# Two layers of linear attention and gated MLP on one core: key reciprocals by logarithm, half sums stored per head, and a written-out order of the work

## The chip, the cores and the metric

The kernel runs on one core of one Trainium2 chip. The time is the device time of one execution in microseconds (us), and lower is better. One execution was also recorded by the hardware profiler; its page and trace are called the profile here. The engines are PE (TensorE, matmuls), DVE (VectorE), ACT (ScalarE), POOL (GpSimd) and SP (SyncE, which here only issues DMAs).

## What is computed

The input x has 2048 rows of 512. Two identical layers follow one another, each an attention block and a gated MLP block, both with a normalisation in front and a residual sum behind. Cut to what matters (H = 32 heads of 16, F = 1376):

```python
q, k, v = heads(x @ wqkv)
pq, pk = q @ w_phi[h], k @ w_phi[h]
phi_q = concat([softmax(pq), softmax(-pq)])      # over the head's 16 features
phi_k = concat([softmax(pk), softmax(-pk)])
kv, z = phi_k.T @ v, phi_k.sum(over rows)        # sums over all 2048 rows
o = (phi_q @ kv) / (phi_q @ z + 1e-6)
x = x + heads_joined(o) @ wo
gate, up = xn @ W_gate, xn @ W_up
x = x + (relu(gate) * up) @ W_down
```

## The kernel before

The 2048 rows lie in 16 tiles of 128, four tiles to a chunk. X stays in SBUF throughout. `Plan` collects some 1800 operations with an engine, a cost, and what they read and write; an operation is one or several instructions. In the kernel before, `Plan.order` (line 99) then walks through simulated time: each engine takes, of its ready operations, the one with the highest rank (the longest remaining way to the end) plus a bias per group from the table `RANK`, as soon as the buffers are free. The order so found is emitted, and on the chip each engine works through its own list in order, waiting on semaphores. So the order on every engine is fixed when the program is built.

The stages of a layer, with the lines of the kernel before:

- **Loads** (lines 225 to 240): key and value weights and some of X on SP's queue, other parts of X, the feature weights and the query weights on ACT's. `load_weights` (line 294) issues the 28 parts of the output and MLP weights on SP.
- **Start** (`wake`, `feature_weights`): three matmuls of zeros (line 318), transposes of the key weight on PE (line 351), products with the feature weights (line 364), evacuated from PSUM by ACT (line 307) or DVE (line 309).
- **Normalisation** (`Norm`): statistics on DVE (lines 388, 390), the reciprocal root on POOL (lines 396, 398), the scaled tile on ACT (line 460), DVE or POOL (line 472), its transpose by DMA from SP (lines 486, 490) or on PE (line 481).
- **Keys and values** (`keys_values`): per tile four matmuls against the key weight (line 710), two exponentials on ACT (line 715; e to the x and e to the -x), their sums per head, the reciprocals of the sums on DVE (line 724), the scaling on POOL or DVE (line 730), the values (line 663, evacuated at 307 or 309), and eight narrow matmuls (line 752) that add the tile to the sums over rows. After the 16th tile DVE builds R from the sums (line 774).
- **Sums per head** (`feature_sums`): 64 numbers per head pair and sign are summed in groups of 16. A letter per tile chooses the way: "1" is one reduction of both signs on DVE (line 682), "2" two reductions (line 692), "H" and "P" let POOL first add the two halves of one or both signs (line 679), and DVE reduces the remainder (line 688).
- **Queries** (`queries`): matmuls (line 794), exponentials (line 798), sums, reciprocal (line 803), product of the reciprocals (line 807), scaling (line 814), transpose by DMA (line 816).
- **Attention** (`attention`): eight narrow matmuls per tile against R (line 833) into the one buffer `q`, a reciprocal (line 851) and a product (line 853) on DVE. That product is called the attention product here; there are 16 per layer. Then a transpose (line 860 or 866, by DMA; line 873 on PE), the output projection (line 884) and the residual sum on DVE (line 566).
- **MLP** (`Centre`, `glu`): centring on ACT or DVE (lines 524, 527), squares on ACT (line 548), transposes (lines 535, 539, 542), matmuls for gate and up (lines 593, 613), their evacuation and product on ACT and DVE (lines 598 to 630), the down projection (line 645), the residual sum (line 566 or, without a running total, 570), and in the last layer the output DMA (line 650). The last tile is stored in three pieces of 256, 128 and 128 columns.

Which engine does what for each tile stands in the strings of `STEP`. Two of its lines, as an example:

```python
    "kr0": "11H11HH11H2211H1", "kr1": "H22P11H2111222PP", "qr0": "21H1H11P2PH11212", "qr1": "112H121HH1HPP12P",
    "qs0": "DPPPDDPDPDPPDDPD", "qs1": "PDPPPPDDPDPPDPPP", "qq0": "DPPPDPDPPDPDDPDP", "qq1": "PPPPDDPDPDPPPPDP",
```

Of the kernel before, what the change touches and what calls it, by code (L numbers as in the profile page):

```python
# [8 lines left out]
P = 128  # L9
D = 512  # L10
H = 32
DH = 16
F = 1376
NDB = D // P
# [36 lines left out]
TAIL = {"PE": 0.165, "ACT": 0.12, "DVE": 0.115, "POOL": 0.045, "SP": 0.0}  # L51
SAME = {"PE": -0.165, "ACT": 0.035, "DVE": 0.035, "POOL": 0.08, "SP": 0.0}
HOPS = {("DVE", "POOL"): 0.09, ("ACT", "POOL"): 0.15}
NEXT = {"PE": 0.055, "SP": 0.03}
FREE = 0.06


def hop(a, b):
    return SAME[a] if a == b else HOPS.get((a, b), NEXT.get(b, 0.04))


class Plan:
# [10 lines left out]
    def op(self, eng, occ, fn, reads=(), writes=(), holds=(), lat=0.0, at=0.0, group=None, port=False, long=False):  # L73

        o = Op()
        o.eng, o.occ, o.cost, o.fn, o.lat, o.at, o.port, o.long = eng, occ, occ + TAIL[eng], fn, lat, at, port, long
        o.group, o.i_in = group or self.group
        base, slope = RANK.get(f"{o.group}.{eng}") or RANK[o.group]
        o.bias = base - slope * o.i_in
        o.preds, o.succs, o.i = set(), [], len(self.ops)  # L80
# [18 lines left out]
    def order(self):  # L99
        for o in self.ops:  # L100
            for p in o.preds:
                p.succs.append(o)
        for o in reversed(self.ops):
            o.rank = o.cost + o.lat + max([s.rank + hop(o.eng, s.eng) for s in o.succs], default=0.0)
        free = {k: [0.0] * n for k, (pool, n) in self.kinds.items()}
        engines = sorted({o.eng for o in self.ops})
        busy = {e: 0.0 for e in engines}
        ready = {e: [] for e in engines}
        for o in self.ops:
            o.wait, o.t0 = len(o.preds), o.at  # L110
            if not o.wait:
                ready[o.eng].append(o)
        seq, left, now, shut = [], len(self.ops), 0.0, 0.0
        while left:
            moved, later = False, []
            for e in engines:
                if busy[e] > now + 1e-9:
                    later.append(busy[e])
                    continue
                best = None  # L120
                for o in ready[e]:
                    if o.t0 > now + 1e-9:
                        later.append(o.t0)
                        continue
                    if o.port and shut > now + 1e-9:
                        later.append(shut)
                        continue
                    ok = True
                    need = {}
                    for b in o.bufs:  # L130
                        if b.slot is None:
                            need[b.kind] = need.get(b.kind, 0) + 1
                    for k, n in need.items():
                        got = [t for t in free[k] if t is not None]
                        if len(got) < n:
                            ok = False
                        else:
                            t = sorted(got)[n - 1]
                            if t > now + 1e-9:
                                later.append(t)  # L140
                                ok = False
                    if ok and (best is None or (o.rank + o.bias, -o.i) > (best.rank + best.bias, -best.i)):
                        best = o
                if best is None:
                    continue
# [5 lines left out]
                if o.long:  # L151
                    shut = end
# [856 lines left out]
```

## Time and profile before

| | |
|---|---|
| Median of 3 runs | 381.89 us (381.57 to 382.64) |
| The profiled execution | 380.91 us |
| Its span, first to last instruction | 379.2 us |
| Granted TensorE clock, mean | 0.999 |
| Busy: PE, DVE, ACT, POOL | 363.6, 268.0, 205.5, 121.1 us |
| DMA traffic | 32.61 MB, mean 86 GB/s |

In the rows of the profile, L12 is line 12 of the kernel of that run. A group's row has the line, the engine, the operation, what it writes and reads, shapes and count; then busy time, the mean time of one in ns, and the idle time before them with what ended it. A timeline's row has the start in us, the duration, the engine, the line, the operation and the count, and in brackets an idle time that preceded it. Successive instructions of an engine overlap a little, so the distance from one start to the next is what an instruction occupies; it is shorter than its duration. Buffer numbers are left out of names: `b` is any work buffer, `ps` a bank of PSUM.

### The profile page before, as it was taken

To read this page: it belongs to the slowest core of one execution; us is meant where nothing else is said; L and a number is where in the kernel's file an instruction comes from. 1 tells how busy PE (TensorE), PEld (TensorE's weight loads), DVE (VectorE), ACT (ScalarE), POOL (GpSimd) and SP (SyncE) were. 2 spreads that over 40 slices of the span, in tenths; PEclk is the share of its full clock that TensorE was granted. 3 is DMA by queue.
4 is the path that set the end of the run, shared out by engine and by line. 5 is a ranking of instruction groups with operands and counts; after the bars stand their busy time and mean duration, and the time that the engine had idled before them with its cause. 6 is when DMAs were issued, how large, how long until landed. Compare 5 with 4: busy or idle time off the path is not lost.

```text
span 379.2 us, 6724 instructions
## 1 busy us (share of the span) xinstructions
PE 363.6 (96%) x2380; PEld 189.9 (50%) x2409; DVE 268.0 (71%) x608; ACT 205.5 (54%) x439; POOL 121.1 (32%) x203
## 2 busy tenths in 40 slices
PE   4898999999899999999999999999999999999996
PEld 2444545756445444444444456475654445454444
DVE  4999999999925442763497998999962675172433
ACT  4898979776762446737706925865234135514100
POOL 3798965131110220560155681724310002000000
PEclk9999999999999999999999999999999999999999
DMA  8889936788950230021013070478930075000011
GB/s 262 239 143 227 260 44 144 133 149 146 145 107 2 42 58 15 0 30 27 0 22 77 9 119 3 87 127 146 171 85 14 5 146 115 14 0 16 1 55 57
DMA packets 98882, 32.61 MB, mean 86 GB/s; under 512 B 90560, under 2 KB 98336, under 8 KB 98848
## 3 DMA queue, kind: packets, MB, share of 16 engines
q1 hardware_dynamic: 97216, 29.93, 39.7%
q10 hardware_dynamic: 1632, 2.24, 1.8%
q8 instruction: 19, 0.31, 0.4%
q14 instruction: 15, 0.12, 0.1%
HBM read 8.44 MB, written 2.10 MB: 28 GB/s over the span
## 4 chain that ended last, share of the span: by engine, by line
PE 64%; DVE 24%; DMA 6%; issue 2%; ACT 1%; POOL 1%; SPq 0%; POOLq 0%; ACTq 0%
PE ps L613 37%; PE ps L645 14%; PE ps L884 5%; DMA b<-b 4%; DVE sk L682 4%; DVE rk L724 3%; DVE bnst L388 3%; PE ps L794 3%; PE ps L593 3%; DVE sk L692 2%; DVE b L730 2%; PE q L833 2%; DMA X<-in_A_x_dram 2%; DVE sq L682 1%; DVE sk L688 1%
## 5 line engine op out<-in xcount | busy, mean ns | idle before, releaser
L613 PE MATMUL ps<-b,wu 128*128 128x512 bf16 (+2 forms) x400 | 79.2, 336 | 0.6 <-DMA b<-b 0.6
L613 PE MATMUL ps<-b,wg 128*128 128x512 bf16 (+2 forms) x400 | 78.6, 336 | 0.0
L645 PE MATMUL ps<-wd,b 128*128 128x512 bf16 (+3 forms) x368 | 78.1, 366 | 0.3
L623 ACT ACTIVATE b<-ps 128x512 bf16<-128x512 f32 (+2 forms) x100 | 50.5, 520 | 39.6 <-PE ps L613 39.1
L626 DVE SCALAR_TENSOR_TENSOR b<-ps,b 128x512 bf16<-128x512 f32 (+2 forms) x60 | 35.1, 598 | 39.9 <-PE ps L613 38.9
L645 PEld LDWEIGHTS <-b 128*128 128x128 bf16 (+1 forms) x374 | 35.3, 98 | 39.1
L613 PEld LDWEIGHTS <-wg 128*128 128x128 bf16 x400 | 36.1, 98 | 33.1
L613 PEld LDWEIGHTS <-wu 128*128 128x128 bf16 x400 | 36.2, 98 | 32.7 <-issue 0.9
L730 POOL TENSOR_TENSOR b<-b,rk 128x1024 bf16<-128x1024 bf16 (+6 forms) x28 | 37.5, 1351 | 9.6 <-DVE rk L724 7.9
L798 ACT ACTIVATE b<-ps 128x512 bf16<-128x512 f32 x64 | 33.0, 638 | 5.7 <-PE ps L794 5.1
L715 ACT ACTIVATE b<-ps 128x512 bf16<-128x512 f32 x64 | 33.7, 628 | 1.3 <-PE ps L710 1.3
L679 POOL TENSOR_TENSOR b<-b 128x256 f32<-128x256 bf16 x30 | 19.7, 670 | 43.9 <-ACT b L715 34.1
L570 DVE SCALAR_TENSOR_TENSOR X<-ps,r,X 128x512 bf16<-128x512 f32 (+2 forms) x26 | 18.2, 701 | 20.2 <-PE ps L645 20.1
L710 PE MATMUL ps<-Wk,b 128*128 128x512 bf16 x123 | 29.4, 379 | 2.0 <-DMA b<-b 1.2
L884 PE MATMUL ps<-wo,b 128*128 128x512 bf16 x118 | 29.7, 379 | 1.5 <-DMA b<-b 0.9
L630 DVE TENSOR_TENSOR b<-b,b 128x512 bf16<-128x512 bf16 (+2 forms) x40 | 13.5, 348 | 24.0 <-ACT b L623 22.3
L552 POOL TENSOR_SCALAR ve<-tot 128x4 f32<-128x4 f32 x8 | 1.9, 233 | 88.8 <-ACT sq L548 88.8
L663 PE MATMUL ps<-wkv,b 128*128 128x512 bf16 x122 | 29.9, 386 | 0.3
L794 PE MATMUL ps<-Wq,b 128*128 128x512 bf16 x126 | 29.5, 379 | 0.1
L548 ACT ACTIVATE sq<-b 128x512 bf16<-128x512 bf16 x32 | 20.1, 627 | 17.4 <-DVE b L527 17.0
L598 ACT CAST ur<-ps 128x192 bf16<-128x192 f32 (+1 forms) x18 | 5.4, 302 | 32.2 <-PE ps L593 32.1
L814 POOL TENSOR_TENSOR b<-b,rq 128x512 bf16<-128x512 bf16 x19 | 20.2, 1061 | 8.4 <-DVE rq L807 6.1
(94 smaller groups left out, 493.7 us busy)
## 6 DMA issues: line engine op xcount, KB each, us to landing
out_dram<-X SPq DMA_DIRECT2D x15, 128.0 KB, 1.8
X<-in_A_x_dram ACTq DMA_DIRECT2D x3, 512.0 KB, 7.2
b<-b SPq DMA_TRANSPOSE x94, 3.2
wg<-in_B_W_gate_dram SPq DMA_DIRECT2D x8, 160.0 KB, 3.2
wu<-in_B_W_up_dram SPq DMA_DIRECT2D x8, 160.0 KB, 4.0
wd<-in_B_W_down_dram SPq DMA_DIRECT2D x5, 256.0 KB, 4.7
wkv<-in_A_wqkv_dram SPq DMA_DIRECT2D x2, 512.0 KB, 7.1
wq<-in_A_wqkv_dram ACTq DMA_DIRECT2D x1, 512.0 KB, 8.3
```

What stands on the lines that cost most here:

```text
L613: nc.tensor.matmul(ps[:], lhsT=wt[:, b, f * P:(f + 1) * P], rhs=xnT[:, lo:hi, b, :], start=(b == 0), stop=(b == NDB - 1))
L623: pl.op("ACT", 0.045 + 0.43 * share, lambda ups=ups, ru=ru, sign=1.0 if fuse else -1.0: nc.scalar.activation(out=ru[:], in_=ups[:], func=A ...
L626: pl.op("DVE", 0.06 + 0.548 * share, lambda gps=gps, ru=ru, h=h, cs=cs: nc.vector.scalar_tensor_tensor(out=h[:, cs], in0=gps[:], scalar=0. ...
L645: nc.tensor.matmul(yps[:], lhsT=hs[f][:fsz, ti * P:(ti + 1) * P], rhs=st.wd[:fsz, f, cols], start=(f == 0), stop=(f == NFT - 1))
L663: nc.tensor.matmul(vp[:], lhsT=xnT[:, ti, kb, :], rhs=st.wkv[:, kb, D:2 * D], start=(kb == 0), stop=(kb == NDB - 1))
L710: nc.tensor.matmul(ps[:], lhsT=xnT[:, ti, kb, :], rhs=w(kb), start=(kb == 0), stop=(kb == NDB - 1))
L715: pl.op("ACT", 0.48, lambda s=s, ek=ek, pk=pk: nc.scalar.activation(out=ek[:, :, s, :], in_=pk[:].rearrange("p (j x) -> p j x", j=8), func ...
L730: eng.tensor_tensor(out=phiK[:, lo:hi, :, :].rearrange("p j s (f h) -> p (j s) f h", h=4), in0=ek[:, lo:hi, :, :].rearrange("p j s (f h) - ...
L794: nc.tensor.matmul(pq[:], lhsT=xnT[:, ti, kb, :], rhs=st.Wq2[:, kb, :], start=(kb == 0), stop=(kb == NDB - 1))
L798: pl.op("ACT", 0.48, lambda s=s, eq=eq, pq=pq: nc.scalar.activation(out=eq[:, :, s, :], in_=pq[:].rearrange("p (j x) -> p j x", j=8), func ...
L814: (nc.vector if on_dve else nc.gpsimd).tensor_tensor(out=e, in0=e, in1=rq[:].unsqueeze(2).to_broadcast([P, 8, DH, 4]), op=Alu.mult)
L884: nc.tensor.matmul(yps[:], lhsT=turned(b), rhs=st.wo[:, b, :], start=(b == 0), stop=(b == NDB - 1))
```

## The change

- The search for an order is replaced by a table, `ORDER`, of 1881 numbers: the operations are emitted in that order, and buffers are given out along it. The costs in the calls of `op` are no longer used for ordering.
- All strings of `STEP` are new: which engine does what for each tile, in how many pieces the first MLP chunk of layer 0 is done (three instead of two), and which transposes PE does.
- A new string, `ki`, chooses for each tile whether DVE takes the key reciprocals, or ACT as exp(-ln(s)) in two instructions (9 tiles in layer 0, 5 in layer 1). `qi` would do the same for queries and is "D" throughout. `rs` does the normalisation's reciprocal root on ACT in the same way for three groups of tiles. One table that holds both functions is loaded at the start.
- POOL's half sums are stored with the eight numbers of a head side by side, instead of four heads interleaved: POOL writes with a step of 32 bytes, and DVE's remainder reads neighbours instead of every fourth number.
- The first loads are issued in another order, three of them as planned operations on ACT's queue.
- 26 instead of 3 matmuls of zeros.
- A path "raw" for the first tiles' keys is added, but it is set to 0 tiles.

The diff, cut to its core:

```diff
@@ Plan.order
-        for o in reversed(self.ops):
-            o.rank = o.cost + o.lat + max([s.rank + hop(o.eng, s.eng) for s in o.succs], default=0.0)
...
+        self.seq = [self.ops[i] for i in ORDER]
+        for at, o in enumerate(self.seq):
+            o.place = at
+            for b in o.bufs:
+                if b.slot is None:
+                    free = [i for i, u in enumerate(owner[b.kind]) if u is None or not u.left]
+                    b.slot = min(free, key=lambda i: last[b.kind][i])
+                    owner[b.kind][b.slot] = b
@@ loads
+LN_EXP = [s.name for s in act_sets.SETS].index("natural_log_exp_and_others")
+LOAD_SP = ((0, 1), (1, 2))
+LOAD_ACT = ("f", "k", (2, 4), "v", (4, 8))
+LATE = ((8, 12), (12, 16), "q")
...
+    nc.scalar.add_instruction(mybir.InstLoadActFuncSet(name=nc.get_next_instruction_name(), act_func_set_id=LN_EXP, ins=[], outs=[]))
     nc.scalar.activation(out=wake[:], in_=st.zero[:, 0:1], func=AF.Exp)
@@ feature_sums
-        halves[s] = Buf("b1", [P, 8, DH // 2, 4], F32)
+        halves[s] = Buf("b1", [P, 8, 4, DH // 2], F32)
 
         def add(s=s, h=halves[s]):
-            x = e[:, :, s, :].rearrange("p j (g y) -> p j g y", g=2)
-            nc.gpsimd.tensor_tensor(out=h[:].rearrange("p j f h -> p j (f h)"), in0=x[:, :, 0, :], in1=x[:, :, 1, :], op=Alu.add)
+            x = e[:, :, s, :].rearrange("p j (g f h) -> p j g f h", g=2, h=4)
+            nc.gpsimd.tensor_tensor(out=h[:].rearrange("p j h f -> p j f h"), in0=x[:, :, 0], in1=x[:, :, 1], op=Alu.add)
...
-                out=sums[:, :, s, :], in_=h[:].rearrange("p j f h -> p j h f"), axis=AX.X, op=Alu.add),
+                out=sums[:, :, s, :], in_=h[:], axis=AX.X, op=Alu.add),
@@ keys_values
+        by_log = STEP["ki" + L][t] == "A"
-        def invert(sk=sk, rk=rk):
+        def invert(sk=sk, rk=rk, by_log=by_log):
+            if by_log:
+                nc.scalar.activation(out=sk[:], in_=sk[:], func=AF.Ln)
+                nc.scalar.activation(out=rk[:], in_=sk[:], func=AF.Exp, scale=-1.0)
+                return
             with nc.allow_low_precision(reason="the reference keeps a softmax and its sums in bfloat16"):
                 nc.vector.reciprocal(out=rk[:], in_=sk[:])
@@ STEP
-    "part0": "4111", "part1": "6111", "tB0": "D---", "tB1": "--DA", "tA": "----", "wev": "ADADAAAAADDAAAAA",
-    "xn1": "ADAADDAPDAADDAAA", "turn": "A-AA", "wake": 3, "fuse0": "AFAA", "fuse1": "FFFF", "gate": 1, "sA": 2,
...
+    "raw": 0, "kev": "ADAD", "ki0": "ADDDDDDAAAADAAAA", "ki1": "DDDDADDDDDAAAADD", "qi0": "DDDDDDDDDDDDDDDD",
+    "qi1": "DDDDDDDDDDDDDDDD", "rs": "APPPPPPAPAPPPPPP", "part0": "3111", "part1": "6111", "tB0": "A---",
+    "tB1": "---A", "tA": "----", "wev": "DADDAAADDDDAAAAA", "xn1": "APADPAAPPAADAAAA", "turn": "ADAA", "wake": 26,
...
+    "ks0": "7087050151860870", "ks1": "4281736108128588", "kr0": "2H2P11H11PH21HH1", "kr1": "21221HP12P1H212H",
+    "qr0": "P2H1H2HPPH2P2H12", "qr1": "21P2111HHH2P1H1P", "qs0": "PPDPPDPPPDPPPDPP", "qs1": "PPDDDPPDPPPDDPPP",
@@ order
-RANK = {
-    "a0.DVE": (-27978.12, 47.27), "a0.PE": (4422.84, 62.03), "a1.DVE": (-3109.09, 76.61), "a1.PE": (-9282.73, -22.35),
...
+ORDER = [int(i) for i in """
+134 142 31 149 155 131 32 141 139 0 40 41 35 33 153 34 143 135 156 148 157 170 171 166 158 162 167 36 147 172 159 49
...
+1864 1865 1877 1866 1867 1868 1873 1874 1810 1811 1812 1869 1870 1871
+""".split()]
```

Lines of the kernel after that the prediction names: L633 is POOL's half sum, L642 its remainder on DVE, L696 and L697 the logarithm and the exponential, L844 the transpose of the attention result behind the attention product at line 837.

More of the change, by code (lines that the diff above doesn't have):

```diff
@@ L47 @@
     pass
[L51 to L59, printed above, removed]
 class Plan:
@@ L296, in load_weights @@
     nc, seen = st.nc, {}
+    st.pl.rank("xl")
+    before = ()
+    for what, issue in st.late:
+        keys = [("wqin", 0)] if what == "q" else [("Xin", t) for t in range(*what)]
+        st.pl.op("ACT", 0.45, issue, reads=list(before), writes=keys, at=3.6, lat=2.0)
+        before = keys[:1]
     for n, (name, dst, src, kb) in enumerate(st.loads):
@@ L865, in attention @@
         elif how == "-":
[L866 to L867 removed]
+            pl.op("SP", 1.29, lambda o=o, oT=oT: nc.sync.dma_start_transpose(out=oT[:], in_=o[:]),
+                  reads=[(o, 0)], writes=[(oT, 0)], lat=1.17)
         else:
```

236 lines of the change are left out of this document (98 added, 138 removed), and 100 rows, old and new, of tables (ORDER, RANK, STEP).

## The prediction

> **What bounds the kernel now.** I read the page first, for the span and the engines' shares.
>
> ```profile
> span 379.2 us, 6724 instructions
> ...
> PE 363.6 (96%) x2380; PEld 189.9 (50%) x2409; DVE 268.0 (71%) x608; ACT 205.5 (54%) x439; POOL 121.1 (32%) x203
> ```
>
> TensorE looks full, but a busy matmul holds its pipeline's latency too. So I price its work by the pace of dense rows, one from the chain and the others from the timeline of PE:
>
> ```profile
> 166.86 17.27 PE ps L613 x80
> ```
> ```profile
> 49.23 1.18 PE L752 MATMUL q<-vext,b 128*128 128x68 bf16 x32
> 50.25 1.03 PE L663 MATMUL ps<-wkv,b 128*128 128x512 bf16 x3
> ...
> 66.77 0.39 PE L613 MATMUL ps<-b,wg 128*128 128x128 bf16 x4
> 66.99 0.39 PE L613 MATMUL ps<-b,wu 128*128 128x128 bf16 x4
> ...
> 79.97 0.49 PE L593 MATMUL ps<-wr,b 128*128 128x192 bf16 x4
> 80.30 0.81 PE L613 MATMUL ps<-b,wu 128*128 128x384 bf16 x4
> 80.94 0.81 PE L613 MATMUL ps<-b,wg 128*128 128x384 bf16 x4
> ```
>
> 17.27/80 = 0.216 us for 512 columns; start to start 0.16 for 384, 0.083 for 192, 0.055 for 128, 0.032 for 68. The listing of the built program holds 1333, 160, 128, 258 and 512 of these (and 18 that are neither wake-ups nor of these widths): about 357 us of work in 379.2. Some 22 us are lost. Where? These rows bound the ends:
>
> ```profile
> 1.24 1.46 PE L318 MATMUL ps<-zero 128*128 128x512 bf16 x3 [1.24 <-DVE zero L234]
> 5.37 1.89 PE L351 MATMUL ps<-ident,wkv 128*128 128x128 bf16 x16 [2.66 <-DMA wkv<-in_A_wqkv_dram]
> ...
> 364.64 11.68 PE L645 MATMUL ps<-wd,b 128*128 128x512 bf16 x74
> ```
>
> 5.4 us pass before the first transposes of the key weight, and 2.9 after the last matmul (376.3 to 379.2). For the rest I asked for stretches of 10 us (columns: the stretch, its length, busy us of PE, PEld, DVE, ACT, POOL, clock, DMA):
>
> ```profile
> 20.00:30.00 10.00, 9.25 (x42) 3.82 (x41) 10.00 (x17) 9.95 (x20) 9.67 (x14) 1.00 0.81 135
> 50.00:60.00 10.00, 9.17 (x72) 4.53 (x72) 10.00 (x22) 7.56 (x17) 7.89 (x13) 1.00 0.62 100
> 80.00:90.00 10.00, 10.00 (x84) 6.32 (x83) 10.00 (x30) 8.36 (x22) 1.30 (x2) 1.00 0.91 146
> 110.00:120.00 10.00, 10.00 (x49) 4.51 (x47) 4.84 (x7) 2.63 (x5) 0.00 (x0) 1.00 0.14 28
> ```
>
> Up to about 100 us VectorE never rests; from 110 TensorE runs at full pace and VectorE idles. To see how tight the first part is I price VectorE the same way, start to start:
>
> ```profile
> 20.95 0.54 DVE L724 RECIPROCAL rk<-sk 128x64 bf16<-128x64 f32 x1
> 21.42 1.15 DVE L682 TENSOR_REDUCE sk<-b 128x64 f32<-128x1024 bf16 x1
> 22.49 0.66 DVE L692 TENSOR_REDUCE sk<-b 128x32 f32<-128x512 bf16 x1
> 23.08 0.53 DVE L724 RECIPROCAL rk<-sk 128x64 bf16<-128x64 f32 x1
> ...
> 52.90 0.77 DVE L774 TENSOR_TENSOR R<-M,q 128x272 bf16<-128x272 bf16 x2
> ...
> 55.53 0.60 DVE L688 TENSOR_REDUCE sq<-b 128x32 f32<-128x256 f32 x1
> 56.05 0.34 DVE L803 RECIPROCAL sq<-sq 128x32 f32<-128x32 f32 x1
> ...
> 75.48 0.71 DVE L853 TENSOR_TENSOR b<-q,dd 128x512 bf16<-128x512 f32 x1
> ...
> 104.31 0.69 DVE L853 TENSOR_TENSOR b<-q,dd 128x512 bf16<-128x512 f32 x1
> ```
>
> That is 0.47 for a key reciprocal, 1.07 for a whole sum (L682), 0.59 for a half (L692), about 0.5 for the rest of a half that GpSimd began (L688: 0.52). With such a price for each form, the listing puts 70.2 us of VectorE work ahead of the 7th attention product of layer 0 (L853, at 75.48) and 98.1 ahead of the 16th (at 104.31). The remainders, 5.3 and 6.2 us, hardly differ: after its first data VectorE simply works through its list. TensorE's list holds 58.7 and 86.6 us ahead of the same products, so it is 17.7 behind the clock at 104.31. Most of the 22 us is lost here, and a small rest in layer 1's attention and at the end.
>
> **The change, part by part.** (1) *Order and shares.* I priced the new listing by the same rows, wake-up matmuls not counted as work:
>
> | ahead of product | VectorE before, after | TensorE before, after | difference before, after |
> |---|---|---|---|
> | 1st | 53.1, 51.5 | 43.3, 45.2 | 9.8, 6.3 |
> | 7th | 70.2, 68.5 | 58.7, 60.3 | 11.5, 8.2 |
> | 8th | 76.0, 72.7 | 62.2, 66.4 | 13.8, 6.3 |
> | 16th | 98.1, 112.6 | 86.6, 124.6 | 11.5, -12.0 |
>
> Up to the 7th product VectorE loses 9 key reciprocals (9 x 0.47 = 4.2), 4 normalisations (1.3) and 6 whole sums, gains 8 half sums of its own, 8 remainders (together +2.2), 1.3 of key scaling and 0.3 of small things: -1.7. The rest is order: after the 8th product the new list gives TensorE 38 us more GLU work ahead of the last products, so from there TensorE is the bound.
>
> VectorE's remainder was 5.3. The same X and weight transfers are issued in another order, and four evacuations (1.3 us) are now in its list where it waited for data. I take 5.0, between 4.0 (all four hidden) and 6.2 (before's own at the 16th). The 7th product then starts at 68.5 + 5.0 = 73.5, TensorE is 73.5 - 60.3 = 13.2 behind instead of 17.7, and keeps that: **4.5 us gained**.
>
> (2) *ScalarE.* 14 key reciprocals become a logarithm and an exponential, 9 of them in layer 0. Rows from the groups by shape and from the timeline of ACT:
>
> ```profile
> L236 ACT ACT_TABLE_LOAD x1 | 1.3, 1283 | 1.7 <-PEq L993 1.7
> L598 ACT CAST ur<-ps 128x96 bf16<-128x96 f32 x4 | 1.0, 249 | 0.3 <-PE ps L593 0.3
> L236 ACT ACTIVATE wake<-zero 128x1 f32<-128x1 bf16 x1 | 0.2, 203 | 0.0
> ```
> ```profile
> 0.79 0.42 ACTq L226 DMA_DIRECT2D X<-in_A_x_dram  x1
> ...
> 24.75 0.81 ACT L460 ACTIVATE b<-X,ve,rstd 128x512 bf16<-128x512 bf16 x1
> 25.48 6.92 ACT L715 ACTIVATE b<-ps 128x512 bf16<-128x512 f32 x14
> ```
>
> No row is 64 wide; a pair lies between 2 x 0.203 and 2 x 0.249; I take 0.45. The listing has one table load in either kernel, so none is added by Ln. Ahead of R (L774), ScalarE's list grows from 40 exponentials, 29 evacuations and 9 normalisations (an evacuation has an exponential's shape: 69 x 0.49 + 9 x 0.73 = 40.4) to 48, 27 and 10, nine pairs, three DMA issues and six tiny ones (75 x 0.49 + 10 x 0.73 + 9 x 0.45 + 3 x 0.42 + 6 x 0.2 = 50.6). It is free of its five first issues, the table load and the wake at 0.8 + 2.1 + 1.3 + 0.2 = 4.4, so at 55.0 at the earliest it has done what R needs. VectorE arrives there at 49.7 + 5.0 = 54.7. The two are level: ScalarE costs nothing in my sum, but nothing covers it any more.
>
> (3) *Half sums.* GpSimd makes 39 instead of 30, 15 instead of 6 ahead of R, and writes them 32 bytes apart; VectorE then reads eight neighbours instead of every fourth number.
>
> ```profile
> L814 POOL TENSOR_TENSOR b<-b,rq 128x512 bf16<-128x512 bf16 x19 | 20.2, 1061 | 8.4 <-DVE rq L807 6.1 <-PE q L833 1.3
> L679 POOL TENSOR_TENSOR b<-b 128x256 f32<-128x256 bf16 x30 | 19.7, 670 | 43.9 <-ACT b L715 34.1 <-ACT b L798 9.6 <-DVE b L626 0.2
> L688 DVE TENSOR_REDUCE sk<-b 128x32 f32<-128x256 f32 x13 | 7.4, 575 | 0.2 <-POOL b L679 0.2
> L472 POOL TENSOR_SCALAR b<-X,mv,rstd 128x512 bf16<-128x512 bf16 x1 | 2.1, 2092 | 0.1
> ```
>
> L688 takes 0.52 for 256 elements, L692 0.59 for 512. At L692's pace the new read would take 0.30, so it saves between 0 and 0.22 each, 20 times before the 7th product: 0 to 4.4. I take half of it, 2.2, and let 1.0 through, since ScalarE is level. GpSimd's new write costs between nothing and 1.42 more (L472's 2.09, the slowest row, against 0.67); I take 0.2, near L814's 1.06 for twice the outputs halved. GpSimd's list ahead of R is 43 us with the old price and 46 with mine; it can start at about 5 and has until 55.
>
> [...]
>
> (4) *Wake-ups.* 26 instead of 3; eleven stand ahead of the first transposes, in the hole from 1.24 to 5.37, at 0.216 to 0.49 each (1.46/3): done between 3.6 and 6.6, so up to 1.2 late. The other 15 (3.2 us) lie where TensorE waits for VectorE by 6 us or more. I cost them at nothing; without that cover they cost 3.2. The transposes ran at 1.89/16 = 0.118 instead of 0.055, so TensorE started slow, but it isn't the bound there. [...]
>
> (5) *What is given back.* Eight more transposes on TensorE: 8 x 0.055 = 0.44. And the end: before, the last piece is 128 columns wide; after, the split tile stands earlier and the last output is a full tile.
>
> ```profile
> 376.36 0.35 DVE L570 SCALAR_TENSOR_TENSOR X<-ps,r,X 128x128 bf16<-128x128 f32 x1 [0.27 <-PE ps L645]
> ```
> ```profile
> out_dram<-X SPq DMA_DIRECT2D x15, 128.0 KB, 1.8
> out_dram<-X SPq DMA_DIRECT2D x2, 32.0 KB, 1.4
> ```
> ```profile
> L570 DVE SCALAR_TENSOR_TENSOR X<-ps,r,X 128x512 bf16<-128x512 f32 x23 | 17.0, 741 | 19.3 <-PE ps L645 19.3
> ```
>
> 0.74 - 0.35 + 1.8 - 1.4 = 0.8 us later. In layer 1 VectorE's lists shrink by 5 and 8 us, but TensorE is the bound there: nothing. GLU's first chunk in three pieces has the same columns. On SP's queue the weight loads now stand between the transposes; the same 28 as before, and the first GLU comes 1.6 us of TensorE work later in the list: nothing.
>
> The sum: the profiled execution took 380.91 (its span 379.2 and 1.7 around it). 380.91 - 4.5 - 1.0 + 0.44 + 0.8 = 376.65. It was 0.98 under the median of 381.89, so **377.6** as a median. Bounds: remainder 4.0 and the whole read saving (-1.0, -3.4) give 373.2; remainder 6.2, no read saving and late transposes (+1.2, +1.0, +1.2) give 381.0.
>
> **The rivals.** *ScalarE becomes the bound.* Its queue is in order: a logarithm that waits for VectorE's sum holds up the exponentials behind it, for which TensorE's banks wait. For it: level at 55 us, 9.95 busy in 20:30. Against: 7.56 in 50:60. If each of the nine pairs holds it for 0.5 us, 4.5 us go and all is given back: 376.65 + 1.0 + 4.5 = 382.1, 383.1 as a median; with 0.3 each 381.3. No change.
>
> *GpSimd's strided write is slow (slower than before).* Ahead of R GpSimd has 55 - 5 - 43 = 7 us to spare. With 15 half sums there, the gain (without the read saving 4.5 less the 1.2 given back: 3.3) is gone when they cost 7 + 3.3 = 10.3 more, 0.69 each: a half sum of 1.36 us. At L472's 2.09 they cost 21.3 more: 381.9 + 21.3 - 10.3 = 393; halfway between the two points 387. [...] Against: L814's write of twice the size takes 1.06.
>
> *More than forecast.* The read saving whole, and the rest of the loss gone as well (22 - 17.7 - 2.9, some 1.5 us, mostly in layer 1): 371.5 to 373.2. *The order doesn't do what it says*: a wait that the listing doesn't show, for a buffer or a transpose, at the 7th product; same time as the first rival.
>
> **How the numbers follow.** Forecast 0.56 (373.2 to 380.7); ScalarE or another wait gives it back 0.15 (380.7 to 383); slow write 0.19 (383 to 393); more than forecast 0.10. A measurement of this kernel tells about 0.3% (1.1 us) from no change: faster 0.66, same 0.15, slower 0.19. The range 372.5 to 385.5 leaves out about half of the slow write's chance and half of the best case.
>
> **What would show it.** In the new trace: the 7th attention product (line 837) near 73.5 us; VectorE continuously busy to there and not to 104; R near 55; L642 near 0.45 in busy time and L633 near 0.87; a Ln-Exp pair near 0.45; an end 3.7 us after the last matmul. It is wrong if TensorE's loss up to the 16th product isn't near 13, if L633 is over 1.3 us, or if ScalarE has no gap before R while VectorE has.

## The result and the profile after

The changed kernel takes 380.13 us (median of 9 executions, 379.3 to 380.86); on the same chip the kernel before takes 383.06 (381.57 to 384.36). The ratio, here and below over all executions but two that ran at a mean granted clock of 0.66 and 0.76 (one of e3 with 552.9 us, one of g3 with 481.4), is 0.994, with a 95% interval of 0.9916 to 0.9964; that of the two medians is 0.992. So the kernel is faster by some 0.6%, where 1.1% was forecast (377.6). The profiled executions stand 0.78 us apart: 380.13 after, 380.91 before. Executions of the kernel before spread from 380.2 to 384.4 us, and its profile is among the faster ones.

The page of the changed kernel, shares of the span and chain of waits:

```profile
span 378.4 us, 6902 instructions
...
PE 368.7 (97%) x2520; PEld 195.5 (52%) x2520; DVE 264.3 (70%) x598; ACT 211.4 (56%) x502; POOL 134.7 (36%) x220
...
PE 80%; POOL 6%; DVE 6%; ACT 3%; DMA 3%; issue 1%; ACTq 0%; POOLq 0%
```

GpSimd (POOL) has 13.6 us more to do than before, and stands in the chain with as large a share as VectorE. The stretches of 10 us show where it became full (columns as in the prediction); first the kernel after, then two rows of before that were not yet shown:

```profile
20.00:30.00 10.00, 9.48 (x64) 4.72 (x65) 9.72 (x20) 10.00 (x21) 9.83 (x11) 1.00 0.73 152
30.00:40.00 10.00, 10.00 (x68) 4.82 (x65) 9.30 (x20) 9.83 (x22) 9.92 (x16) 1.00 0.61 121
40.00:50.00 10.00, 9.82 (x80) 4.80 (x78) 9.33 (x17) 9.79 (x24) 9.92 (x13) 1.00 0.83 221
50.00:60.00 10.00, 8.72 (x100) 4.93 (x97) 9.65 (x19) 8.83 (x22) 9.51 (x11) 1.00 0.99 192
```
```profile
30.00:40.00 10.00, 9.35 (x91) 5.18 (x92) 10.00 (x20) 8.57 (x17) 8.43 (x11) 1.00 0.97 236
40.00:50.00 10.00, 9.95 (x103) 5.74 (x101) 10.00 (x20) 9.68 (x21) 8.32 (x8) 1.00 0.68 206
```

Before, VectorE was at 10.00 in each of these rows and GpSimd at 7.9 to 9.7. After, GpSimd is at 9.5 to 9.9 and VectorE has gaps of 0.3 to 0.7 in each. ScalarE is nearly full as well. R and the products that the forecast was tied to, in VectorE's timeline:

```profile
57.95 0.78 DVE L750 TENSOR_TENSOR R<-M,q 128x272 bf16<-128x272 bf16 x2
...
78.75 0.67 DVE L837 TENSOR_TENSOR b<-q,dd 128x512 bf16<-128x512 f32 x1
...
141.25 0.69 DVE L837 TENSOR_TENSOR b<-q,dd 128x512 bf16<-128x512 f32 x1
```

R came at 57.95 (forecast near 55, before 52.90), the 7th product at 78.75 (forecast 73.5), and at the 16th TensorE is 141.25 - 124.6 = 16.7 us behind its work instead of 17.7: 1.0 us gained, not the 4.5 of step (1), nor the 5.5 with the 1.0 that step (3) let through.

### The profile page after: what moved, and what is told of

The parts are those of the page before. It is cut to its first block, busy times and chain, and to the rows that moved or that the text cites. A ratio compares the mean times of both kernels' runs of the same rounds, so it can differ in the third digit from the quotient of the medians.

```text
span 378.4 us, 6902 instructions
## 1 busy us (share of the span) xinstructions
PE 368.7 (97%) x2520; PEld 195.5 (52%) x2520; DVE 264.3 (70%) x598; ACT 211.4 (56%) x502; POOL 134.7 (36%) x220
## 4 chain that ended last, share of the span: by engine, by line
PE 80%; POOL 6%; DVE 6%; ACT 3%; DMA 3%; issue 1%; ACTq 0%; POOLq 0%
PE ps L567 35%; PE ps L599 19%; PE ps L868 7%; PE ps L770 5%; PE ps L617 4%; PE ps L664 4%; PE ps L547 3%; POOL b L706 2%; PE q L817 2%; DMA X<-in_A_x_dram 2%; DVE b L706 2%; DMA b<-b 1%; POOL b L633 1%; PE q L728 1%; POOL b L426 1%; ACT b L685 1%
## 5 line engine op out<-in xcount | busy, mean ns | idle before, releaser
L567 PE MATMUL ps<-b,wu 128*128 128x512 bf16 (+3 forms) x440 | 82.1, 321 | 0.0
L567 PE MATMUL ps<-b,wg 128*128 128x512 bf16 (+3 forms) x440 | 82.0, 321 | 0.0
L577 ACT ACTIVATE b<-ps 128x512 bf16<-128x512 f32 (+3 forms) x110 | 50.4, 484 | 55.4 <-PE ps L567 55.0
L706 POOL TENSOR_TENSOR b<-b,rk 128x1024 bf16<-128x1024 bf16 (+7 forms) x26 | 35.0, 1357 | 27.4 <-DVE rk L700 9.5
L774 ACT ACTIVATE b<-ps 128x512 bf16<-128x512 f32 x64 | 36.1, 619 | 11.9 <-PE ps L770 11.9
L685 ACT ACTIVATE b<-ps 128x512 bf16<-128x512 f32 x64 | 36.9, 632 | 6.0 <-PE ps L664 5.8
L633 POOL TENSOR_TENSOR b<-b 128x256 f32<-128x256 bf16 x39 | 27.1, 704 | 36.6 <-ACT b L774 17.2
L524 DVE SCALAR_TENSOR_TENSOR X<-ps,r,X 128x512 bf16<-128x512 f32 (+2 forms) x22 | 14.9, 698 | 25.3 <-PE ps L599 25.3
L520 DVE SCALAR_TENSOR_TENSOR X<-ps,X 128x512 bf16<-128x512 f32 x32 | 21.8, 682 | 11.4 <-PE ps L868 11.4
L798 POOL TENSOR_TENSOR b<-b,rq 128x512 bf16<-128x512 bf16 x22 | 23.6, 1077 | 3.5 <-DVE rq L791 2.6
L584 DVE TENSOR_TENSOR b<-b,b 128x128 bf16<-128x128 bf16 (+2 forms) x50 | 18.4, 399 | 8.0 <-ACT b L577 4.5
```

The lines of the kernel that those rows point to most:

```text
L567: nc.tensor.matmul(ps[:], lhsT=wt[:, b, f * P:(f + 1) * P], rhs=xnT[:, lo:hi, b, :], start=(b == 0), stop=(b == NDB - 1))
L577: pl.op("ACT", 0.045 + 0.43 * share, lambda ups=ups, ru=ru, sign=1.0 if fuse else -1.0: nc.scalar.activation(out=ru[:], in_=ups[:], func=A ...
L633: nc.gpsimd.tensor_tensor(out=h[:].rearrange("p j h f -> p j f h"), in0=x[:, :, 0], in1=x[:, :, 1], op=Alu.add)
L685: pl.op("ACT", 0.48, lambda s=s, ek=ek, pk=pk: nc.scalar.activation(out=ek[:, :, s, :], in_=pk[:].rearrange("p (j x) -> p j x", j=8), func ...
L706: eng.tensor_tensor(out=phiK[:, lo:hi, :, :].rearrange("p j s (f h) -> p (j s) f h", h=4), in0=ek[:, lo:hi, :, :].rearrange("p j s (f h) - ...
L774: pl.op("ACT", 0.48, lambda s=s, eq=eq, pq=pq: nc.scalar.activation(out=eq[:, :, s, :], in_=pq[:].rearrange("p (j x) -> p j x", j=8), func ...
```

## The experiments

All edits are made to the changed kernel unless said. "R" and "16th" are starts in VectorE's timeline (L750, L837); the time of the kernel before is of the same chip. Two more profiles whose layer 0 is that of the changed kernel (h1 and f1, below) have R at 57.66 and 57.62, so a difference of 0.3 us in R says nothing.

| run | R | 16th | median us | before | ratio, 95% interval |
|---|---|---|---|---|---|
| changed kernel | 57.95 | 141.25 | 380.13 | 383.06 | 0.994 (0.9916 to 0.9964) |
| e1 old half layout | 57.09 | 141.2 | 380.49 | 382.38 | 0.9934 (0.9916 to 0.9951) |
| e2 four norms to VectorE | 59.14 | 142.4 | 381.19 | 382.38 | 0.9964 (0.9941 to 0.9987) |
| e3 key reciprocals on VectorE | 59.91 | 143.7 | 382.45 | 382.38 | 0.9988 (0.9967 to 1.0008) |
| e6 short sums, VectorE | 57.71 | 141.6 | 380.54 | 381.96 | 0.9967 (0.9949 to 0.9985) |
| e9 short sums, both | 56.11 | 139.9 | 379.29 | 381.96 | 0.9937 (0.9916 to 0.9958) |
| e7 no logarithm | 58.27 | 141.6 | 380.24 | 381.96 | 0.9965 (0.9952 to 0.9979) |
| f2 key shares | 56.20 | 139.8 | 378.67 | 382.40 | 0.9911 (0.9888 to 0.9933) |
| f4 short halves, no logarithm | 54.84 | 139.2 | 378.64 | 382.40 | 0.9913 (0.9887 to 0.9938) |
| f1 split tile last | 57.62 | 140.8 | 379.54 | 382.40 | 0.9938 (0.9915 to 0.9962) |
| g4 shares and end | 56.20 | 139.6 | 377.77 | 382.41 | 0.9889 (0.9864 to 0.9915) |

**The layout of the half sums alone (e1, e4).** e1 puts the old layout back; e4 gives the new one to the kernel before.

```diff
-        halves[s] = Buf("b1", [P, 8, 4, DH // 2], F32)
+        halves[s] = Buf("b1", [P, 8, DH // 2, 4], F32)
```

> The changed kernel, with the half sums laid out as before the change (the four heads' numbers interleaved); order, shares, logarithm and wake-ups as changed. Theories: (A) ahead of R GpSimd's list sets the pace, because it got nine more half sums and three more normalisations; (B) ScalarE's list does, because of the logarithm pairs in its in-order queue; (C) VectorE still does, as I forecast. All: the remainder (L642) goes back from 0.40 to about 0.57 us, the half sum (L633) stays at 0.67 to 0.70. C: 20 remainders ahead of the 7th attention product cost 20 x 0.17 = 3.4 us, so the kernel is 3 us slower than the changed one (about 383). A and B: VectorE has gaps that hide most of it; 0 to 1 us slower (380 to 381).

> The kernel before, with the new layout of the half sums alone. In it VectorE never rests up to 104 us, and 12 to 13 remainders of layer 0 lie in its list. If VectorE's list sets that kernel's pace, the remainders fall from 0.57 to 0.40 us and it is 12 x 0.17 = 2 us faster than before (381); with the start to start saving of up to 0.33 each 4 us (379). If GpSimd or ScalarE sets the pace there too, 0 to 1 us faster (382 to 383).

e1 took 380.49 us, e4 380.86 beside 382.38 for before (0.996, 0.9938 to 0.9983), 1.5 us faster. By form, in the changed kernel (its remainders, its half sums) and in before (the same; columns: count, shortest, median and longest in ns, first and last start):

```profile
L642 DVE TENSOR_REDUCE sk<-b x16: 355/404/420, 18.1 to 222.7; 128x32 f32<-128x256 f32 x16
```
```profile
L633 POOL TENSOR_TENSOR b<-b x39: 667/674/1117, 16.7 to 262.2; 128x256 f32<-128x256 bf16 x39
```
```profile
L688 DVE TENSOR_REDUCE sq<-b x17: 496/587/623, 52.4 to 268.3; 128x32 f32<-128x256 f32 x17
```
```profile
L679 POOL TENSOR_TENSOR b<-b x30: 661/667/750, 20.1 to 251.4; 128x256 f32<-128x256 bf16 x30
```

The read became 0.18 us cheaper, the write 7 ns dearer. In the kernel before this is worth 1.5 us, in the order of what 12 remainders save (12 x 0.18 = 2.2); but e4's profile has the 16th product at 104.4 as before and only the 17th earlier (235.2 for 236.4), so that the gain comes from VectorE's list of layer 0 is not shown. In the changed kernel the layout is worth nothing that can be measured: with the old one the ratio is 0.9934 instead of 0.994, and R comes 0.5 to 0.9 us earlier, not later.

**Work moved between engines (e2, e3).**

```diff
-"xn1": "APADPAAPPAADAAAA"
+"xn1": "ADADDAADDAADAAAA"
```
```diff
-"ki0": "ADDDDDDAAAADAAAA"
+"ki0": "DDDDDDDDDDDDDDDD"
```

> The changed kernel, with the four tile normalisations that GpSimd does ahead of R (L426, 2.09 us each) done by VectorE instead (about 0.32 each); nothing else. A: GpSimd's list ahead of R shrinks by 8.4 us, VectorE's grows by 1.3; R comes 3 to 5 us earlier than 57.95 and the kernel is 2 to 4 us faster than the changed one (376 to 378). B: R stays at about 58, same time (379.5 to 380.5). C: 1.3 us slower (381.4).

> The changed kernel, with layer 0's nine key reciprocals that ScalarE does by logarithm and exponential put back on VectorE; nothing else. ScalarE's list ahead of R shrinks by 9 x 0.48 = 4.3 us, VectorE's grows by 9 x 0.47 = 4.2. A: R not earlier, 0 to 2 us slower, as VectorE's gaps (about 5 us) take most of it (380 to 382). B: R 2 to 4 us earlier, 1 to 3 us faster (377 to 379). C: 4 us slower (384).

Neither helped. e3's profile came 2 us later at R, and its median is about 2 us longer, at the upper end of what theory A gave. Much of that is TensorE's clock, which was 0.50 from 58 to 60 us in that profile (last section): the three executions with a mean clock of 0.998 or more took 380.0, 380.3 and 381.5 us, the eight with 0.993 to 0.996 took 382.2 to 383.9. So with the clock held, moving the nine reciprocals back costs between nothing and 1.4 us. e2 went against A at first sight: 8.4 us off GpSimd's list, and R 1.2 later. Its waits say why (GpSimd from 17 to 56 us, then VectorE from 12 to 58):

```profile
POOL ve L345 <- DVE mv L333: 6.0, 2, 4.9
```
```profile
DVE b L426 <- POOL rstd L351: 1.3, 1, 1.3
```

GpSimd, with the normalisations gone, ran ahead and waited for VectorE's statistics, and a normalisation in VectorE's in-order list waited for GpSimd's root. What was taken off its list before 30 us turned into waiting, and from 30 us on it was as full as ever (9.92 in each row to 50). To tell the engines apart, work had to go from one without coming to another.

**One engine relieved at a time (e6, e9, e7, f4).** These leave work out.

```diff
# e6 and e9: layer 0's sums read a quarter; e9 adds the two lines for GpSimd's half sums
+    w = 16 if group in ("h0", "i0") else 4 * DH
-    in_=e[:, :, s, :].rearrange("p j (f h) -> p j h f", h=4)
+    in_=e[:, :, s, 0:w].rearrange("p j (f h) -> p j h f", h=4)
...
-        halves[s] = Buf("b1", [P, 8, 4, DH // 2], F32)
+        halves[s] = Buf("b1", [P, 8, 4, w // 8], F32)
-            x = e[:, :, s, :].rearrange("p j (g f h) -> p j g f h", g=2, h=4)
+            x = e[:, :, s, 0:w].rearrange("p j (g f h) -> p j g f h", g=2, h=4)
# e7: without layer 0's logarithm; f4: e7 with e9's two lines for the half sums
-                nc.scalar.activation(out=sk[:], in_=sk[:], func=AF.Ln)
+                if L == "1":
+                    nc.scalar.activation(out=sk[:], in_=sk[:], func=AF.Ln)
```

> The changed kernel, with the sums of layer 0 (L636, L642, L646) reading only a quarter of their input, so that the denominators are wrong; GpSimd's half sums stay whole. Takes some 0.7, 0.15 and 0.3 us from each on VectorE, ahead of R about 7 x 0.7 + 14 x 0.15 + 17 x 0.3 = 12 us; ScalarE, GpSimd and TensorE keep their lists. If VectorE sets the pace, R comes 8 us or more earlier than 57.95 and the kernel is 4 us or more faster (376 or less). If GpSimd's list (full from 17 us) does, R comes 0 to 2 us earlier, and 0 to 1.5 us faster. If ScalarE's list (full from 12 to 50 us) does, the same.

> As the run with short sums on VectorE, and GpSimd's half sums of layer 0 also add only a quarter of their input (128x64 instead of 128x256, about 0.4 us less each, 9 to 10 of them ahead of R: 4 us). Beside the run with VectorE's sums alone it tells GpSimd from ScalarE: if GpSimd's list sets the pace, R comes a further 3 to 4 us earlier; if ScalarE's or TensorE's does, not.

> The changed kernel, with the logarithm of layer 0's nine pairs left out (the exponential alone is kept, so the reciprocals are wrong). ScalarE's list ahead of R is 9 x 0.2 = 1.9 us shorter, VectorE's and GpSimd's are the same. If ScalarE sets the pace (my first rival), R comes 1.5 us earlier and the kernel is 1 to 1.9 us faster (378.5); if another engine does, within 0.5 of 380.1.

> The changed kernel, with GpSimd's half sums of layer 0 adding only a quarter of their input (VectorE's remainders read that quarter) and the logarithm of layer 0's pairs left out; VectorE's whole and half sums as they were, so the reciprocals are wrong. GpSimd's list ahead of R is 4.5 us shorter, ScalarE's 1.9, VectorE's 2. If GpSimd's list sets the pace and ScalarE's the next: R at 54 to 55.5 (57.95 in the changed kernel, 56.1 with both VectorE's and GpSimd's sums short), 1.5 to 2.5 us faster (377.6 to 378.6). If something else holds R (transfers, the chain of the sums): R at 56 or later, less than 1 us faster.

e6 is the clearest. Two of its stretches, its R, and VectorE's waits from 12 to 58 us (the kernel has one line more, so R is L751 and the remainders L643):

```profile
30.00:40.00 10.00, 9.89 (x61) 4.70 (x60) 4.71 (x16) 9.94 (x23) 9.92 (x16) 1.00 0.68 125
40.00:50.00 10.00, 9.77 (x83) 4.90 (x83) 7.69 (x18) 9.79 (x25) 9.92 (x13) 1.00 0.83 218
```
```profile
57.71 0.78 DVE L751 TENSOR_TENSOR R<-M,q 128x272 bf16<-128x272 bf16 x2
```
```profile
DVE sk L637 <- ACT b L686: 2.8, 2, 1.9
DVE sq L643 <- POOL b L634: 2.6, 2, 2.2
DVE rk L701 <- POOL b L707: 1.9, 1, 1.9
DVE sk L643 <- POOL b L634: 1.9, 4, 0.8
```

VectorE falls from 9.30 busy to 4.71, and R stays. The freed time became waits for GpSimd (half sums, key scaling) and for ScalarE's exponentials. e7 takes the logarithm off ScalarE: R at 58.27, no gain either. GpSimd has no wait between 17 and 56 us in either. With its half sums short as well (e9), it begins to wait, mostly for ScalarE,

```profile
POOL b L634 <- ACT b L775: 2.1, 3, 1.2
POOL b L634 <- ACT b L686: 2.1, 4, 1.1
POOL b L707 <- ACT rk L698: 1.2, 1, 1.2
```

and R comes at 56.11: 1.6 us earlier than in e6, not the 3 to 4 expected for GpSimd alone; its waits are now for ScalarE. In f4, with both shorter and VectorE's sums whole but for the remainders, R comes at 54.84, and the 16th product 2.0 us earlier.

So it is GpSimd's load that holds R, with ScalarE's list next. How it holds R shows in VectorE's last three key scalings, of 1024, 1024 and 128 columns, the last VectorE work that R needs. In the changed kernel, e6, e9 and e3:

```profile
54.85 2.54 DVE L706 TENSOR_TENSOR b<-b,rk 128x1024 bf16<-128x1024 bf16 x3
```
```profile
53.86 3.29 DVE L707 TENSOR_TENSOR b<-b,rk 128x1024 bf16<-128x1024 bf16 x3 [0.73 <-ACT rk L698]
```
```profile
53.22 1.49 DVE L707 TENSOR_TENSOR b<-b,rk 128x1024 bf16<-128x1024 bf16 x3 [0.74 <-ACT rk L698]
```
```profile
57.13 1.43 DVE L706 TENSOR_TENSOR b<-b,rk 128x1024 bf16<-128x1024 bf16 x3
```

In the changed kernel and in e6 GpSimd works beside all three, in e9 beside the first and the start of the second, in e3 beside none (from 50 to 58 us it is busy for 7.57, 7.50, 7.15 and 6.20). The same work takes VectorE 1.4 to 1.5 us or 2.5 to 3.3. From e6 to e9 the three start 0.6 us earlier and are 1.8 shorter, and 0.8 of it goes to a wait for TensorE: 1.6. In e6 the work taken off VectorE let them start 1.0 us earlier than in the changed kernel, and GpSimd beside them took most of that away again. So R comes late not only for what GpSimd itself has to finish, but also because VectorE's work beside it took longer (2.54 and 3.29 us instead of 1.43 and 1.49; but 1.42 in e1, where GpSimd is busy for 7.92 of those 8 us and R comes at 57.09).

**Key scaling moved off GpSimd (f2), ScalarE next (g3).** A real change, with all the work in it:

```diff
-"ks0": "7087050151860870"
+"ks0": "4085040141840850"
```

> The changed kernel, with 11 of the 64-column pairs of layer 0's key scaling moved from GpSimd to VectorE (shares 4 5 4 4 4 5 instead of 7 7 5 5 6 7 of 8): GpSimd's list ahead of R 11 x 0.2165 = 2.4 us shorter, VectorE's 11 x 0.0735 = 0.8 longer. If GpSimd's list sets the pace with ScalarE's 1 to 2 us behind it: R 1 to 2 us earlier than 57.95, and 0.5 to 1.2 us faster (379 to 379.6). If VectorE sets it: 0.8 slower (381).

R at 56.20, and 378.67 us: 0.9911 of before. VectorE's longer list costs nothing: from one start to the next, its key scalings ahead of R occupy 7.8 us for 9728 columns, where the changed kernel's occupy 8.6 for 8320; the last three take 1.57 us instead of 2.54, and from 50 to 58 us GpSimd is busy for 6.76 instead of 7.57. VectorE then waits for TensorE's last key sums:

```profile
56.20 0.79 DVE L750 TENSOR_TENSOR R<-M,q 128x272 bf16<-128x272 bf16 x2 [0.67 <-PE q L728]
```

g3 adds the split tile at the end (below) and `"ev0": "AAAAAADAAADAAAAA"`, two evacuations from ScalarE to VectorE.

> As the run with shares and end, and two of ScalarE's sixteen evacuations of values of layer 0 (0.48 each) done by VectorE (0.55 each). If ScalarE's list is the next bound behind GpSimd's, R comes 0.5 to 1 us earlier and the kernel is 0.3 to 0.9 us faster; if VectorE's is level with it, the same or up to 1 us slower.

R came at 57.08, 0.9 us later than in f2 and g4, and the time was 378.27 (0.9893, 0.9869 to 0.9917): no gain over g4's 377.77. So with the shares moved, taking work off ScalarE for VectorE gains nothing; that R moves by about the 1.1 us by which VectorE's list grew speaks for VectorE as level with the pace then.

**The end (f1, g4).** The last tile's three pieces (operations 1872 to 1880) are put back to the end of `ORDER`; g4 has f2's shares as well.

```diff
-1814 1815 1806 1863 1808 1880 1809 1875 1872 1876 1864 1865 1877 1866 ... 1812 1869 1870 1871
+1814 1815 1806 1863 1808 1809 1864 1865 1866 ... 1812 1869 1870 1871 1872 1873 1874 1875 1876 1877 1878 1879 1880
```

> The changed kernel, with the last output tile's pieces of 256, 128 and 128 columns put back to the very end of the list; nothing else. My step (5) priced the end at 0.8 us, the traces at 0.7 (3.57 after the last matmul instead of 2.88): 0.7 us faster (379.4), with 2.9 after the last matmul. If the end is hidden or was mispriced: within 0.3 of the changed kernel.

> The changed kernel with the key shares moved and the split tile last. If the two effects (1.5 and 0.6 us in single runs) are of separate places, they add: 377.8 to 378.2 us. If not, 378.7.

f1 took 379.54, 0.6 less than the changed kernel, though on another chip. It has the small piece last again, but its span of 377.7 still ends 3.4 us after the last matmul (374.3), not 2.9:

```profile
374.36 0.35 DVE L524 SCALAR_TENSOR_TENSOR X<-ps,r,X 128x128 bf16<-128x128 f32 x1 [0.27 <-PE ps L599]
```

g4 took 377.77; its span ends 3.1 us after the last matmul (375.9 - 372.8), f2's without the edit 3.6 (376.7 - 373.1). In the other profiles with the edit (f3, g2 and h2, below) it is 2.9, 2.9 and 3.4. The end is worth 0.2 to 0.7. To set it beside the changed kernel on one chip, both ran again:

> The changed kernel itself, to stand beside the run with key shares and end on the same chip: 380.1 us, 0.994 of before.

> The run with key shares and end again, beside the changed kernel: if GpSimd's list (1.5 us) and the end (0.6) are the causes, 1.8 to 2.4 us faster than it. If the earlier difference came from the chips, less than 1 us.

379.95 (379.53 to 380.43) and 378.56 (378.2 to 379.19); before took 382.07, ratios 0.9942 (0.9926 to 0.9958) and 0.9906 (0.9889 to 0.9924). The version beats both kernels: the changed one by 1.4 us on the same chip, less than the 1.8 to 2.4 that the single effects add up to.

**The late wake-ups (e5, f3, g1, g2).** Fifteen of the 26 matmuls of zeros are left out; f3 has f2's shares and f1's end as well.

```diff
-nc.tensor.matmul(z[:], lhsT=st.zero[:, 0:P], rhs=st.zero[:], start=True, stop=True),
+nc.tensor.matmul(z[:], lhsT=st.zero[:, 0:P], rhs=st.zero[:], start=True, stop=True) if i < 11 else None,   # g1, g2: if i in (1, 4, 5, 9, 11, 12, 13, 18, 19, 23, 25)
```

> The changed kernel with 11 wake-up matmuls, those ahead of the first transposes; the 15 that stand later in TensorE's list (15 x 0.216 = 3.2 us) are left out. Theory P: TensorE's own in-order list has become nearly full up to R (its idle time from 10 to 60 us is only some 4 us in the changed kernel), so the late wake-ups that I costed at nothing stand on the path: 2 to 3.2 us faster (377 to 378). Theory V (VectorE, GpSimd and ScalarE set the pace, TensorE waits for them): TensorE idles for the time instead, within 0.7 of 380.1; or slower, if the clock drops without them.

> The changed kernel with three edits at once: the key shares moved, the 15 late wake-ups left out, the split tile last. The sum of the single effects would be 0.5 to 1.2 + 0 to 0.7 + 0.7 = 1.2 to 2.6 us faster than the changed one (377.5 to 378.9), which would beat both kernels.

In both, the matmuls were left out by their number in the program, not by their place in the list: only four stood ahead of the first transposes and seven later. So these two (380.33, ratio 0.9952, and 378.68, 0.9916) don't test the late ones alone; in e5 the lack of seven early ones costs nothing visible (R at 57.78), while f3, on another chip, is 0.9 us behind g4. g1 and g2 leave out the right fifteen, g2 on top of g4:

> The changed kernel with the eleven wake-up matmuls that stand ahead of the first transposes, and without the 15 later ones (15 x 0.216 = 3.2 us of TensorE). My step (4) has them hidden: within 0.5 of the changed kernel. If TensorE's own list is the pace up to R: 2 to 3.2 us faster.

> As the run with shares and end, and without the 15 late wake-ups. Hidden wake-ups: the same within 0.5. On the path: 2 to 3.2 us faster.

g1 took 379.50 (0.9929, 0.9907 to 0.9951), g2 379.03 (0.9898, 0.9873 to 0.9924). The late wake-ups are not on the path by anything near 2 to 3.2 us: without them the time is 0.6 us shorter in g1 and 1.3 longer in g2. Why longer shows in g2's single executions: the two with a mean clock of 1.0 took 377.1 and 377.4 us, some 0.5 less than g4, the four with 0.994 or 0.995 took 379.0 to 379.2, and the profiled one is of these. Its TensorE, and its stretches of 2 us (the clock is the third number from the end):

```profile
17.79 0.28 PE L307 MATMUL ps<-Wblk,b 128*128 128x128 bf16 x2
20.18 0.95 PE L307 MATMUL ps<-Wblk,b 128*128 128x128 bf16 x14 [2.11 <-DMA b<-wq]
21.42 4.45 PE L664 MATMUL ps<-Wk,b 128*128 128x512 bf16 x11 [0.28 <-DMA b<-b]
```
```profile
20.00:22.00 2.00, 1.40 (x16) 1.05 (x18) 2.00 (x5) 2.00 (x5) 2.00 (x2) 0.94 0.55 117
22.00:24.00 2.00, 2.00 (x5) 0.71 (x5) 2.00 (x7) 1.62 (x4) 1.92 (x2) 0.50 0.59 113
24.00:26.00 2.00, 2.00 (x8) 0.82 (x7) 1.09 (x4) 1.37 (x4) 1.92 (x5) 0.70 0.85 223
```

TensorE waited 2.1 us for the transposed query weight, and its clock then fell to half (0.94, 0.50 and 0.70 in the three stretches; at 0.50 that is 2 x (0.06 + 0.50 + 0.30) / 0.50 = 3.4 us, an estimate); R came at 58.03 instead of 56.20. In g1's profile the same wait was 1.8 us and the clock stayed at 1.00, but four of its other five executions have a mean clock of 0.993 to 0.995. Of the 39 executions of the kernels that keep all 26 wake-ups and do the same work (the changed one twice, f1, f2, g4, h2) none is under 0.998.

## Why the prediction was wrong

The sign was right and the size was not: 0.78 us between the profiled executions instead of 4.3 (2.9 between the medians beside each other, 2.1 when both ran again). What the slower executions of the kernel before lose, no trace here shows; the sums below explain the 0.78.

**The step that failed** is the spare time of GpSimd in step (3): "GpSimd's list ahead of R is 43 us with the old price ... it can start at about 5 and has until 55", "7 us to spare". On it stood step (1), in which VectorE's list plus a remainder of 5.0 gave the 7th product at 73.5. The runs showed that the list has no spare time: from 17 to 56 us GpSimd never waits. Its busy time up to R (a stretch of GpSimd alone: length, then busy us), and some of its forms from 5 to 58 us (busy us, mean ns of one):

```profile
0.00:58.00 58.00, 50.05 (x77) 1.00 0.78 184
```
```profile
L633 POOL TENSOR_TENSOR b<-b 128x256 f32<-128x256 bf16 x16 | 11.4, 724 | 0.0
L426 POOL TENSOR_SCALAR b<-X,mv,rstd 128x512 bf16<-128x512 bf16 x4 | 8.3, 2089 | 0.1
...
L351 POOL TENSOR_TENSOR rstd<-ve,mhalf 128x2 f32<-128x2 f32 x5 | 3.7, 742 | 0.1
L400 POOL TENSOR_SCALAR u<-mv 128x2 f32<-128x2 f32 x7 | 2.3, 340 | 0.3
L791 POOL TENSOR_TENSOR rq<-sq 128x32 bf16<-128x32 f32 x5 | 2.3, 465 | 0.4 <-DVE sq L786 0.4
```

50 us busy instead of 43: the small operations on 1, 2 or 32 columns are dear (0.19 to 0.74 each, 12.0 in all), and some half sums were held for 0.4 us (longest 1117 ns instead of 667). How the seven divide is not shown. GpSimd also waited 4.7 us for VectorE's statistics before 17 us. 50.05 and 7.9 us of waits and gaps fill the span to R. The order had given it nine or ten more half sums and three more normalisations than before, so VectorE's work was saved where GpSimd's was added. e6 shows that VectorE's own work wasn't the pace, f2 and e9 that GpSimd's was.

On the same step hangs a term that the prediction left out: what a GpSimd without spare time costs VectorE. Step (1) added 1.3 us of key scaling to VectorE's list. From one start to the next, the key scalings ahead of R occupied 4.1 us before and 8.6 after: 3.1 more than the 5.4 that this gives, and about what R was late by. VectorE itself waited only 1.9 us from 12 to 58. So in the changed kernel VectorE was nearly always busy up to R, as forecast, but part of its work was slower. This term alone doesn't set R either: f4 has 8.9 us of it and R at 54.84. How much of the 3.3 us is held time on VectorE and how much GpSimd's own list stays open.

**Step by step.** (1) R 3.3 us late (57.95 for 54.7) is most of the 3.5 that TensorE's lag is off (16.7 for 13.2). From R to the 7th product it took 20.8 us, not 18.8: VectorE waited 1.6 us there for TensorE and ScalarE, which the forecast had left out. Even f4, with R at the 54.8 that I had forecast, ran the 16th product at 139.2, a lag of 14.6 and not 13.2.

(2) The pair was priced well: 0.46 from one to the next instruction (37.30 to 37.76), 0.45 forecast.

```profile
37.30 0.27 ACT L696 ACTIVATE sk<-sk 128x64 f32<-128x64 f32 x1
37.59 0.26 ACT L697 ACTIVATE rk<-sk 128x64 bf16<-128x64 f32 x1
37.76 1.06 ACT L250 CAST vext<-ps 128x512 bf16<-128x512 f32 x2
```

No table load was added: the profiles of both kernels have one, of 1.3 us. With GpSimd relieved, ScalarE lets R come at 56.1 (e9), 1.1 later than my 55.0; e7 shows that it isn't the first bound. The rival of ScalarE had the right kind of mechanism, the wrong engine. Its sign did appear: from 12 to 58 us ScalarE waited 0.3 us and VectorE 1.9. By e7 that sign alone did not make ScalarE the bound.

(3) The read saved 0.18 by its duration (587 to 404 ns), inside 0 to 0.22, where I took half. The write, 32 bytes apart, cost next to nothing, where I took 0.2: 674 ns instead of 667. So the rival of the slow write fell by its price; yet the point from which it decides, 7 us of spare time, was wrong too: with none to spare a write of 0.2 more would already have cost.

(4) The late wake-ups cost some 0.5 us, not 3.2 (g1, and g2 at full clock). Behind the early ones the transposes were faster:

```profile
5.95 1.07 PE L294 MATMUL ps<-ident,wkv 128*128 128x128 bf16 x16 [0.40 <-DMA wkv<-in_A_wqkv_dram]
```

1.07/16 = 0.067 us for a transpose (1.39/16 = 0.087 in f2's profile) instead of 0.118, though e5, with only four of the eleven, loses nothing clear by that. What I missed is the clock: without the late ones, four of six executions of g1 and four of six of g2 had a mean clock of 0.993 to 0.995.

(5) The last output landed 378.4 - 374.83 = 3.6 us after the last matmul instead of 2.9: 0.7 for the 0.8 forecast. Putting the small piece last gave between 0.2 (f1) and 0.7 (f3, g2) of it back. TensorE's listed work grew by 0.6 us, forecast 0.44. (Of the 18 further matmuls in the prediction's count for before, three are the wake-ups; its sum of 357 stands.)

The sum that came out: of the lag at the last matmul, before 376.3 - 356.6 = 19.7 us and after 374.8 - 357.2 = 17.6 (the work priced from the listings as in the prediction), 2.1 are gained, 1.0 in layer 0 and 1.1 later; 0.6 more work and 0.7 at the end leave 0.8. The later part is what "More than forecast" named: counted by the matmuls that had started, layer 1's attention lost 2.7 us before and 1.7 after.

Two things follow. The sign was in part luck: the sum put layer 1 at nothing, and without its 1.1 the 1.3 given back would have outweighed layer 0's 1.0. And layer 0's 1.0 is not the new order's. Counted in the same way, TensorE was 11.1 us behind its listed work at 20 us before, 10.1 after; from there to the end of layer 0's attention it lost 5.8 before and 5.7 after (5.4 in h1). (29 matmuls that before's trace lacks are counted by their weight loads.) So nearly all of it was won in the first 20 us, and the new order and shares gained next to nothing behind that. What won it is not shown; e5 and f3, with fewer early wake-ups, are at 10.1 and 9.9 there too.

## What to carry to other kernels

Where one engine never rests, ask of every other engine in the same stage what its list costs up to the same point, with its smallest operations and its waits in it, before a gain on the first is booked. Price the work that two engines do side by side from rows in which both are busy: a free price for the one can be wrong once the other has no gaps (here three key scalings of 1.43 us took 2.54 and 3.29). A rebalancing gains only down to the next full list; here, moving 2.4 us of work from GpSimd to VectorE gained 1.5. Filler matmuls that stand in waits can be worth keeping for the clock alone: without 15 of them, four of g2's six executions had a mean clock of 0.994 or 0.995 and took 379.0 to 379.2 us, the two at 1.0 took 377.1 and 377.4.

## What the runs showed of the hardware

VectorE's key scaling and GpSimd's work took longer side by side in some profiles. The three last key scalings above took 1.43 us in e3, where GpSimd is busy for 0.44 of the 2 us from 56 to 58, and 2.54 and 3.29 with it busy beside them (the changed kernel, e6). In e1 they took 1.42 with GpSimd busy for 7.92 of the 8 us from 50 to 58, so that it is busy is not enough; which of its work lengthens them is not shown. Another group, VectorE in the changed kernel, then GpSimd at the same time:

```profile
41.86 3.02 DVE L706 TENSOR_TENSOR b<-b,rk 128x384 bf16<-128x384 bf16 x3
```
```profile
41.94 1.38 POOL L706 TENSOR_TENSOR b<-b,rk 128x640 bf16<-128x640 bf16 x1
43.28 1.06 POOL L633 TENSOR_TENSOR b<-b 128x256 f32<-128x256 bf16 x1
44.29 0.70 POOL L791 TENSOR_TENSOR rq<-sq 128x32 bf16<-128x32 f32 x1
44.95 0.67 POOL L633 TENSOR_TENSOR b<-b 128x256 f32<-128x256 bf16 x1
```

Three of VectorE's multiplications (384, 896 and 1024 columns) take 3.0 us, and GpSimd's half sum and small product beside them 1.06 and 0.70 instead of 0.67 and 0.25 (the medians of all 39 and all 26 in that profile). How much of GpSimd's 50 us is held time stays open: an estimate from the means above is 16 x (0.724 - 0.667) + 5 x (0.465 - 0.25) = 2.0 us in its half sums and small products.

TensorE's clock fell to 0.50 after a wait of 2.1 us in g2's profile, and not after 1.8 us in g1's; where it fell in g1's other executions is not shown, so these two don't give a threshold. In e3 it fell after one of 2.5:

```profile
57.88 2.00 PE L728 MATMUL q<-vext,b 128*128 128x68 bf16 x32 [2.46 <-DVE b L706]
```
```profile
58.00:60.00 2.00, 2.00 (x33) 1.82 (x33) 1.12 (x5) 0.00 (x0) 1.02 (x2) 0.50 0.77 257
```
